# Attention ahead of a routed two-layer network: products with v later in the step, their diagonal part a step later, three probability buffers

## The chip, the cores and the metric

One Trainium2 chip, one of its cores. The metric is device time in microseconds (us) of one execution. TensorE (PE, with its weight loads as PEld), VectorE (DVE), ScalarE (ACT) and GpSimd (POOL) each run their instructions in the order in which they were issued; SyncE (SP) and the queues of ACT and POOL issue transfers (DMA). The order on each engine is written out by hand; waits between engines are semaphores.

## The reference

```python
def _attn_ref(q, k, v):                    # q, k, v: 8 batches, 8 heads, 576 rows, 64 wide
    scores = 1.0 / np.sqrt(D) * np.matmul(q, k.transpose(0, 1, 3, 2))
    mask = block_i >= block_j              # blocks of 64 rows
    scores = np.where(mask, scores, -1000000000.0)
    attn = np.exp(scores - np.max(scores, axis=-1, keepdims=True))
    attn = attn / (np.sum(attn, axis=-1, keepdims=True) + 1e-09)
    return np.matmul(attn, v)

def _moe_ref(x, domain_id, w1, w2):        # x: 4608 x 512, 8 experts, 512 -> 1024 -> 512
    for e in range(E):
        mask = domain_id == e
        out[mask] = np.maximum(x[mask] @ w1[e], 0.0) @ w2[e]
    return out
```

The attention's output, laid out as 4608 rows of 512, is x of the second part.

## The kernel before

**Pairs.** The 64 heads are worked in 32 pairs (two heads, t = 0 and 1, side by side on 64 partitions each); four pairs are a batch. Of a pair, the scores are made transposed (keys on partitions) in three groups of one PSUM tile `ps` each (two buffers, two banks each): G0, G1 and G2 (`emit_G0`, `emit_G1`, `emit_G2`), each followed by one exp on ACT (`emit_exp`, L375) that writes 1024 columns of f16 probabilities into the buffer `A` of the pair (two buffers, `As`). G0 holds the keys of block column 0, G1 those of 1, G2 those of 2 and 3; the tail (rows 512 to 575 against keys 512 to 575, a 64 x 64 product for each head, L386) is written into G0's tile.

**Products with v.** `emit_P` (L412) makes 20 products of 128 x 128 probabilities with 65 columns of v (the first column is ones, so the sums come out as well) into the PSUM tile `po`; `emit_D` (L424) makes the 10 products of the diagonal blocks: 8 of 64 x 64 and, last, two of the tail (64 x 128). `emit_N` (L433, L434) divides on DVE out of `po` into `x`; `store_x` (L443, L444) sends x to `xd` in DRAM, once a batch, and for the last batch in two pieces.

**Turning q and k.** q and k are loaded as they lie (`load_qk`, four buffers, POOL's queue) and turned on PE by 18 transposes for two pairs of one of them (`emit_T`, L359) into the PSUM tile `PT` (one buffer), which DVE copies (L362) into `QK` (two buffers).

**Order.** In the loop `for p in range(npair + 1)` PE gets, in step p: G1(p), P(p - 1), D(p - 1), G2(p), G0(p + 1), and then one T; DVE gets the division of pair p - 1, the copy of T and one piece of `routing()`, the work that sorts the rows by expert. In step 23 the sorting's last products (`inv_mm`, 36 of them, L220) and `inv_close` stand after G0. The v and q, k of later batches are asked for in the first step of a batch.

**Into the second part.** Weights are loaded from step 22 on by the same POOL queue. `early_gather` (steps 24 to 26 and 28 to 30) fetches rows of x that lie in the first five batches for the first two experts; `early_block` (steps 30, 31 and 32, L476, into `PT`) turns the three blocks of the first expert. After the loop `mm1` (L601) and `mm2` (L618) work the experts one by one; the rest of the rows (`gather`, L462) is fetched when all of x has been stored. `transpose_block` turns these blocks, and everything after them follows on PE.

Of the kernel before, what the change touches and what calls it, by code (L numbers as in the profile page):

```python
# [17 lines left out]
def kernel(  # L18
# [10 lines left out]
    nc = tc.nc  # L29
# [34 lines left out]
    kh = [asb.tile([128, HP, S], F16, name=f"kh{i}") for i in range(RV)]  # L64
    As = [asb.tile([128, 2, 64 + 3 * 512], F16, name=f"A{i}") for i in range(2)]
    vS = [asb.tile([128, 5, H, 80], F16, name=f"vS{i}") for i in range(RV)]
# [93 lines left out]
    for i in range(RV):  # L160
        nc.vector.memset(vS[i][:, :, :, 15:16], 1.0)
    for i in range(2):
        nc.vector.memset(As[i][:, :, 0:64], 0.0)

# [167 lines left out]
    def new_QK(G):  # L332
        QKs[G] = asb.tile([128, 2, 2, S], F16, name="QK", tag="QK", bufs=2)

# [44 lines left out]

    def emit_G0(st):  # L380
        ps, QK, i = new_ps(), st["QK"], st["i"]
        st["A"] = As[st["p"] % 2]
# [8 lines left out]
    def emit_G1(st):  # L391
        ps = new_ps()
        mm_qk(ps[:, :, 0:64], st, 0, 512, 576)
        mm_qk(ps[:, :, 64:512], st, 1, 128, 576)
        emit_exp(st["A"][:, :, 576:1088], ps[:])
# [10 lines left out]
    def emit_P(st):  # L406
        b = st["p"] // HP
        for w in range(4):
            for t in range(2):
                for c in range(w + 1):  # L410
                    n0 = (128, 576, 896, 1088)[c] + 128 * w
                    nc.tensor.matmul(  # L412
                        out=po[:, t, 65 * w : 65 * w + 65],
                        lhsT=st["A"][:, t, n0 : n0 + 128],
                        rhs=vS[b % RV][:, c, head(st, t), 15:80],
                        start=(w == 0), stop=False)

    def emit_D(st):
        b = st["p"] // HP
        for w, c, n0, k in ((0, 1, 640, 0), (1, 2, 1088, 0), (2, 3, 1408, 0),  # L420
                            (4, 0, 64, 0), (3, 4, 0, 64)):
            r0 = 0 if k else 64
            for t in range(2):
                nc.tensor.matmul(  # L424
                    out=po[r0:128, t, 65 * w : 65 * w + 65],
                    lhsT=st["A"][k : k + 64, t, n0 : n0 + 128 - r0],
                    rhs=vS[b % RV][k : k + 64, c, head(st, t), 15:80],
                    start=False, stop=(w == 3))

    def emit_N(st):  # L430
        c0 = 256 * (st["p"] % HP // 2)
        rc = asb.tile([128, 2, 5], F32, name="rc", tag="rc", bufs=2)
# [22 lines left out]
    def new_pair(p):  # L455
        st = {"p": p, "i": p % 2, "QK": QKs[p // 2]}
        emit_G0(st)
        return st
# [43 lines left out]
    new_QK(1)  # L502
    T_ahead = {0: (1, 0)}
    T_mid = {1: (1, 1)}
    T_end = {}
    for p in range(1, npair):
        G = (p + 3) // 2
        if G < npair // 2:
            T_end[p] = (G, 1 - p % 2)
    prev = None  # L510

    def tok_of(e):
        return tok0[:, :, NB * e : NB * e + NB]

    for p in range(npair + 1):
        b, hp = divmod(p, HP)
        st, nxt = nxt, None
        if st is not None:
            if hp == 0:
                x_t = asb.tile([128, 5, DM], F16, name="x", tag="x", bufs=2)  # L520
            st["x"] = x_t
            emit_G1(st)
        if prev is not None:
            emit_P(prev)
        if p in T_mid:
            emit_T(*T_mid[p])
        if prev is not None:
            emit_D(prev)
        if st is not None:
            emit_G2(st)  # L530
            if p in T_ahead:
                emit_T(*T_ahead[p])
            if p + 1 < npair:
                nxt = new_pair(p + 1)
        if prev is not None:
            emit_N(prev)
            if prev["p"] == npair - 2:
                store_x(prev, 0, DM - 192, nc.sync)
            elif prev["p"] == npair - 1:
                store_x(prev, DM - 192, DM, nc.scalar)  # L540
            elif prev["p"] % HP == HP - 1:
                store_x(prev, 0, DM, nc.sync)
        if p == 1:
            next(rout)
        if p == 23:
            pv = po[:, 0, 325 : 325 + 2 * E * NB].rearrange("p (a c) -> p a c", a=2)
            inv_mm(inv, pv)
            inv_close(asb, pv, E * NB, tok0[:])
        if p in T_end:
            G, s = T_end[p]  # L550
            if s == 0 and G > 1:
                new_QK(G)
            emit_T(G, s)
        if hp == 0 and 1 <= b < B - 3:
            load_v_chunks(b + 3, 0, H, range(5))
        if p >= 1 and hp == (b == 0) and b + 4 < B:
            load_qk(b + 4, 0, HP)
        if p > 1:
# [179 lines left out]
```

## Time and profile before

| | |
|---|---|
| median of 3 runs | 279.83 us (279.24 to 280.53) |
| the profiled execution | 280.8 us, its span 278.7 us |
| busy in the span | PE 255.0 (91%), PEld 167.1, DVE 136.6, ACT 140.2, POOL 157.4 us |
| mean granted TensorE clock | 0.97 of full speed |
| POOL's DMA queue | 59936 packets, 45.63 MB, 96.3% of 16 engines' span |

A span is the time from the first to the last instruction. The attention fills the first 117 us, with ACT, DVE and PE all busy nine tenths of the time; from 130 us on PE alone is busy, without a gap until the last expert. Idle time of an engine counts where the next work waits for it; the view of an engine in order of time gives, in brackets, how long it stood before an instruction and what ended that.

### The profile page before, as it was taken

To read this page: it belongs to the slowest core of one execution; us is meant where nothing else is said; L and a number is where in the kernel's file an instruction comes from. 1 tells how busy PE (TensorE), PEld (TensorE's weight loads), DVE (VectorE), ACT (ScalarE), POOL (GpSimd) and SP (SyncE) were. 2 spreads that over 40 slices of the span, in tenths; PEclk is the share of its full clock that TensorE was granted. 3 is DMA by queue.
4 is the path that set the end of the run, shared out by engine and by line. 5 is a ranking of instruction groups with operands and counts; after the bars stand their busy time and mean duration, and the time that the engine had idled before them with its cause. 6 is when DMAs were issued, how large, how long until landed. Compare 5 with 4: busy or idle time off the path is not lost. (4 is left out here: it accounts for less than half of the span.)

```text
span 278.7 us, 7091 instructions
## 1 busy us (share of the span) xinstructions
PE 255.0 (91%) x3010; PEld 167.1 (60%) x3010; DVE 136.6 (49%) x257; ACT 140.2 (50%) x170; POOL 157.4 (56%) x184
## 2 busy tenths in 40 slices
PE   7599999999999998797999999999999999999940
PEld 5367766777776776554675575665755656657410
DVE  4657999999997976404133404214033042250220
ACT  1747989999997899450352160340521604406200
POOL 8696474553635463108748767687776877051240
PEclk9858999999999999999999999999999999999995
DMA  6999999999999999954997999999999996021030
GB/s 85 153 151 170 193 220 194 216 204 194 225 181 229 186 236 248 238 151 83 201 263 155 211 252 217 278 161 243 223 223 281 189 228 250 25 110 59 38 136 2
DMA packets 65585, 50.86 MB, mean 183 GB/s; under 512 B 40973, under 2 KB 53773, under 8 KB 65552
## 3 DMA queue, kind: packets, MB, share of 16 engines
q0 software_dynamic: 59936, 45.63, 96.3%
q1 hardware_dynamic: 5088, 4.56, 6.0%
q8 instruction: 25, 0.41, 0.5%
q10 hardware_dynamic: 528, 0.20, 0.3%
q14 instruction: 8, 0.07, 0.1%
HBM read 67.15 MB, written 15.20 MB: 296 GB/s over the span
## 5 line engine op out<-in xcount | busy, mean ns | idle before, releaser
L375 ACT ACTIVATE A<-ps 128x1024 f16<-128x1024 f32 x96 | 91.9, 1024 | 15.2 <-PE ps L370 13.4
L605 ACT ACTIVATE hT<-ph 128x640 f16<-128x640 f32 (+2 forms) x72 | 46.4, 644 | 98.6 <-PE ph L601 94.9
L618 PE MATMUL po<-w2h,hT 128*128 128x512 f16 x320 | 74.9, 379 | 0.0
L601 PE MATMUL ph<-xT,w1h 128*128 128x320 f16 (+2 forms) x512 | 71.8, 299 | 1.3 <-DVE xT L479 1.2
L601 PEld LDWEIGHTS <-w1h 128*128 128x128 f16 x512 | 50.0, 98 | 22.8 <-issue 2.4
L628 POOL DMA_INDIRECT out_dram<-osb,tok x40 | 40.4, 1010 | 35.1 <-DVE osb L627 22.5
L479 DVE COPY xT<-pt 128x512 f16<-128x512 f16 x37 | 15.5, 424 | 89.2 <-PE pt L476 89.2
L462 POOL DMA_INDIRECT xg<-x_rows,tok x34 | 34.3, 1010 | 25.3 <-DMA x_rows<-x 12.1
L618 PEld LDWEIGHTS <-hT 128*128 128x128 f16 x320 | 29.9, 98 | 29.5
L94 POOL DMA_DIRECT2D vS<-in_v_dram x40 | 33.2, 839 | 20.1 <-DMA kh<-in_k_dram 8.5
L362 DVE COPY QK<-PT 128x1152 f16<-128x1152 f16 x30 | 40.7, 1356 | 6.8 <-PE PT L359 5.4
L370 PE MATMUL ps<-QK 64*128 64x512 f16 (+4 forms) x320 | 38.6, 300 | 4.0 <-ACT A L375 1.8
L627 DVE COPY osb<-po 128x512 f32<-128x512 f32 x40 | 27.4, 684 | 19.4 <-PE po L618 19.4
L412 PE MATMUL po<-vS,A 128*128 128x65 f16 x640 | 26.4, 198 | 1.4 <-DVE x L434 0.8
L412 PEld LDWEIGHTS <-A 128*128 128x128 f16 x640 | 22.5, 100 | 8.6 <-issue 6.8
L434 DVE TENSOR_TENSOR x<-po,rc 128x640 f16<-128x640 f32 x32 | 26.4, 824 | 1.1
L370 PEld LDWEIGHTS <-QK 64*128 64x128 f16 x320 | 16.8, 95 | 11.5 <-issue 6.0
L424 PE MATMUL po<-vS,A 64*64 64x65 f16 (+1 forms) x320 | 20.0, 199 | 0.0
L476 PEld LDWEIGHTS <-xg 128*128 128x128 f16 x160 | 11.7, 98 | 9.5 <-DMA xg<-x_rows,tok 2.4
L424 PEld LDWEIGHTS <-A 64*64 64x64 f16 (+1 forms) x320 | 14.5, 108 | 3.3 <-issue 0.2
L476 PE MATMUL pt<-identh,xg 128*128 128x128 f16 x148 | 14.0, 219 | 2.0 <-DMA xg<-x_rows,tok 2.0
L123 POOL DMA_DIRECT2D w1h<-in_moe_w_dram x16 | 12.2, 766 | 5.8 <-PE ph L601 2.6
(98 smaller groups left out, 140.4 us busy)
## 6 DMA issues: line engine op xcount, KB each, us to landing
w1h<-in_moe_w_dram POOLq DMA_DIRECT2D x16, 512.0 KB, 7.9
w2h<-in_moe_w_dram POOLq DMA_DIRECT2D x16, 512.0 KB, 10.2
vS<-in_v_dram POOLq DMA_DIRECT2D x28, 128.0 KB, 11.8
x_rows<-x SPq DMA_DIRECT2D x7, 512.0 KB, 10.9
qh<-in_q_dram POOLq DMA_DIRECT2D x6, 576.0 KB, 13.8
kh<-in_k_dram POOLq DMA_DIRECT2D x6, 576.0 KB, 13.8
vS<-in_v_dram POOLq DMA_DIRECT2D x16, 64.0 KB, 7.4
qh<-in_q_dram POOLq DMA_DIRECT2D x3, 288.0 KB, 6.9
```

Of the source, the lines that this page charges most:

```text
L94: nc.gpsimd.dma_start(out=vS[b % RV][r0:128, c, h0:h1, 16:80], in_=v[b, h0:h1, 128 * c : 128 * c + n, :].rearrange("h p d -> p h d"))
L362: nc.vector.tensor_copy(out=QKs[G][:, s].rearrange("p i (n j) -> p i n j", j=R), in_=P16.rearrange("p (j i n) -> p i n j", j=R, i=2))
L370: nc.tensor.matmul(out=o[:, t], lhsT=QK[h, 1, i, 128 * c : 128 * c + 128], rhs=QK[h, 0, i, q0:q1], start=True, stop=True)
L375: nc.scalar.activation(out=o, in_=i, func=AF.Exp, scale=0.125)
L412: nc.tensor.matmul(out=po[:, t, 65 * w : 65 * w + 65], lhsT=st["A"][:, t, n0 : n0 + 128], rhs=vS[b % RV][:, c, head(st, t), 15:80], start= ...
L424: nc.tensor.matmul(out=po[r0:128, t, 65 * w : 65 * w + 65], lhsT=st["A"][k : k + 64, t, n0 : n0 + 128 - r0], rhs=vS[b % RV][k : k + 64, c, ...
L462: nc.gpsimd.indirect_dma_start(out=g[:, blk, :], out_offset=None, in_=xd, in_offset=bass.IndirectOffsetOnAxis(ap=tok[:, 1, blk : blk + 1], ...
L601: nc.tensor.matmul(out=ph[:, i, 0:w], lhsT=w1_cols(w1h, dc, fc), rhs=xT[:, dc, c0 : c0 + w], start=(dc == 0), stop=(dc == 3))
L605: nc.scalar.activation(out=hT[:, fc, n0 : n0 + k * w].rearrange("p (i n) -> p i n", i=k), in_=ph[:, 0:k, 0:w], func=AF.Relu)
L618: nc.tensor.matmul(out=po[:], lhsT=hT[:, fc, 128 * blk : 128 * blk + 128], rhs=w2h[:, fc, :], start=(fc == 0), stop=(fc == 7))
L627: nc.vector.tensor_copy(out=osb[:], in_=po[:])
L628: nc.gpsimd.indirect_dma_start(out=dst[blk], out_offset=bass.IndirectOffsetOnAxis(ap=tok[:, 0, blk : blk + 1], axis=0), in_=osb[:], in_off ...
```

## The change

The products with v of pair p - 1 (P) move from between G1(p) and G2(p) to behind G0(p + 1); their diagonal part (D) and the division move into the step after: the two tail products open the step, ahead of G1, and the eight diagonal ones follow G1. The tail scores move from G0's tile into G1's, right ahead of the diagonal products; G0 takes columns 64 to 575 and G1 the first 64. T moves from the end of the step to between the diagonal products and G2. `As` and `QK` get a third buffer. The loop has one step more, the division and each `store_x` come a step later, the loads of v, q and k are asked for in the second step of a batch, `early_block` stands in steps 29 to 31, behind P. The last pair's output lies in `PT` rather than `po`, with a memset of its unused corner.

PE, in a step of the steady loop, before, from the transposes T on (kh, qh: loaded k and q; QK: turned; A: probabilities; equal rows between are left out):

```order
L359 MATMUL PT<-identh,kh_78 64x128
L370 MATMUL ps<-QK 128x64
...
L370 MATMUL ps<-QK 128x448
L412 MATMUL po<-vS_84,A_80 128x65
...
L424 MATMUL po<-vS_84,A_80 64x65
...
L424 MATMUL po<-vS_84,A_80 128x65
L370 MATMUL ps<-QK 128x320
...
L370 MATMUL ps<-QK 128x512
L386 MATMUL ps<-QK 64x64
```

and with the change:

```order
L412 MATMUL po<-vS_84,A_82 128x65
...
L423 MATMUL po<-vS_84,A_82 128x65
L370 MATMUL ps<-QK 128x64
...
L370 MATMUL ps<-QK 128x448
L392 MATMUL ps<-QK 64x64
L423 MATMUL po<-vS_84,A_82 64x65
...
L359 MATMUL PT<-identh,qh_74 64x128
...
L370 MATMUL ps<-QK 128x320
...
L370 MATMUL ps<-QK 128x512
L412 MATMUL po<-vS_84,A_80 128x65
```

P has left the place between G1 (128x448) and G2 (128x320); there now stand the tail scores, the diagonal products and T.

PE, at the end of the attention, before, from G2 of the last pair on (xg: fetched rows that `early_block` turns; w1h: weights of the first expert):

```order
L370 MATMUL ps<-QK 128x192
L476 MATMUL PT<-identh,xg 128x128
L412 MATMUL po<-vS_85,A_81 128x65
...
L424 MATMUL po<-vS_85,A_81 64x65
L424 MATMUL po<-vS_85,A_81 128x65
...
L476 MATMUL PT<-identh,xg 128x128
L601 MATMUL ph<-xT,w1h 128x384
```

and with the change:

```order
L370 MATMUL ps<-QK 128x192
L412 MATMUL po<-vS_86,A_80 128x65
...
L479 MATMUL PT<-identh,xg 128x128
L423 MATMUL po<-vS_86,A_80 128x65
L423 MATMUL po<-vS_86,A_80 64x65
L412 MATMUL PT<-vS_86,A_81 128x65
L423 MATMUL PT<-vS_86,A_81 128x65
L423 MATMUL PT<-vS_86,A_81 64x65
L612 MATMUL ph<-xT,w1h 128x384
```

Two pairs' products with v now stand behind the last G2, and the last block to be turned stands between them.

The core of the diff:

```diff
@@ buffers
-    As = [... for i in range(2)]          QK bufs=2
+    As = [... for i in range(3)]          QK bufs=3
@@ emit_G0, emit_G1
     def emit_G0(st):
-        mm_qk(ps[:], st, 0, 0, 512)
-        (two tail products into ps[64:128, t, 0:64])
-        emit_exp(st["A"][:, :, 64:576], ps[:])
+        mm_qk(ps[:], st, 0, 64, 576)
+        emit_exp(st["A"][:, :, 0:512], ps[:])
     def emit_G1(st):
-        mm_qk(ps[:, :, 0:64], st, 0, 512, 576)
+        mm_qk(ps[:, :, 0:64], st, 0, 0, 64)
         mm_qk(ps[:, :, 64:512], st, 1, 128, 576)
+        (two tail products into ps[64:128, t, 0:64])
         emit_exp(st["A"][:, :, 576:1088], ps[:])
@@ emit_D(st, parts)
+    D_last = ((3, 4, 512, 64),)
+    D_diag = ((0, 1, 640, 0), (1, 2, 1088, 0), (2, 3, 1408, 0), (4, 0, 576, 0))
@@ the loop
-    for p in range(npair + 1):
+    for p in range(npair + 2):
+        if pp is not None:
+            emit_D(pp, D_last)
         if st is not None:
             emit_G1(st)
-        if prev is not None:
-            emit_P(prev)
-        if prev is not None:
-            emit_D(prev)
+        if pp is not None:
+            emit_D(pp, D_diag)
+            emit_N(pp)
+            (store_x of pp as before of prev)
+        turn_qk(p, 0)
         if st is not None:
             emit_G2(st)
             if p + 1 < npair:
                 nxt = new_pair(p + 1)
-        if prev is not None:
-            emit_N(prev)
         (p == 23: inv_mm, inv_close)
-        if p in T_end:
-            emit_T(G, s)
-        if hp == 0 and 1 <= b < B - 3:
-            load_v_chunks(b + 3, 0, H, range(5))
+        if prev is not None and p > 1:
+            if p == npair:
+                prev["po"] = new_PT()[0].rearrange("p (t c) -> p t c", t=2)
+                nc.vector.memset(prev["po"][0:64, :, 260:325], 1.0)
+            emit_P(prev)
+        if hp == 1:
+            if 1 <= b < B - 3:
+                load_v_chunks(b + 3, 0, H, range(5))
+            if b + 4 < B:
+                load_qk(b + 4, 0, HP)
-        if 30 <= p < 30 + NE:
-            early_block(p - 30, new_PT()[0][:, 0:256])
-        prev = st
+        if 29 <= p < 29 + NE:
+            early_block(p - 29, new_PT()[0][:, 0:256])
+        prev, pp = st, prev
```

## Rows read from the trace of the kernel before

**Rows 1.** ACT in order of time: start, length, instruction, [idle before, releaser].

```profile
34.98 2.85 ACT L375 ACTIVATE A<-ps 128x1024 f16<-128x1024 f32 x3 [0.19 <-PE ps L370]
...
62.91 2.86 ACT L375 ACTIVATE A<-ps 128x1024 f16<-128x1024 f32 x3 [0.19 <-PE ps L370]
...
81.19 2.86 ACT L375 ACTIVATE A<-ps 128x1024 f16<-128x1024 f32 x3 [0.19 <-PE ps L370]
...
107.53 2.85 ACT L375 ACTIVATE A<-ps 128x1024 f16<-128x1024 f32 x3 [0.19 <-PE ps L370]
```

**Rows 2.** PE in order of time, one step; columns as in rows 1.

```profile
63.09 0.22 PE L386 MATMUL ps<-QK 64*64 64x64 f16 x2
63.24 0.69 PE L359 MATMUL PT<-identh,qh 128*64 128x128 f16 x18
63.98 0.40 PE L370 MATMUL ps<-QK 64*128 64x64 f16 x4
64.31 0.79 PE L412 MATMUL po<-vS,A 128*128 128x65 f16 x20
65.03 0.58 PE L424 MATMUL po<-vS,A 64*64 64x65 f16 x9
65.42 0.31 PE L370 MATMUL ps<-QK 64*128 64x320 f16 x1
```

**Rows 3.** Busy time by stretch: stretch, length, engines, granted clock, DMA share, GB/s.

```profile
13.00:22.00 9.00, 8.05 (x109) 5.98 (x109) 4.76 (x10) 4.44 (x5) 8.72 (x12) 0.50 1.41 155
24.00:60.00 36.00, 34.82 (x700) 25.42 (x696) 33.89 (x55) 33.20 (x36) 19.27 (x24) 1.00 1.67 199
```

**Rows 4.** Issues on POOL, SP and ACT in order of time; columns as in rows 1.

```profile
23.23 0.74 POOL L75 DMA_DIRECT2D kh<-in_k_dram  x1 [0.66 <-DMA qh<-in_q_dram]
...
63.91 0.76 POOL L75 DMA_DIRECT2D qh<-in_q_dram  x1
...
79.59 0.59 SPq L444 DMA_DIRECT2D x_rows<-x  x1
...
95.31 1.09 POOL L488 DMA_INDIRECT xg<-x_rows,row  x1 [0.66 <-DVE rc L433]
...
116.94 0.41 ACTq L444 DMA_DIRECT2D x_rows<-x  x1
```

**Rows 5.** Transfers of single stretches: what, queue, count, KB each, us to landing.

```profile
kh<-in_k_dram POOLq DMA_DIRECT2D x1, 576.0 KB, 11.5
...
qh<-in_q_dram POOLq DMA_DIRECT2D x1, 576.0 KB, 15.1
...
x_rows<-x SPq DMA_DIRECT2D x7, 512.0 KB, 10.9
...
xg<-x_rows,row POOLq DMA_INDIRECT x1, 13.5
...
x_rows<-x ACTq DMA_DIRECT2D x1, 192.0 KB, 7.3
...
xg<-x_rows,tok POOLq DMA_INDIRECT x4, 2.8
```

**Rows 6.** PE in order of time, from the attention's end into the experts.

```profile
110.91 0.40 PE L476 MATMUL PT<-identh,xg 128*128 128x128 f16 x4
...
114.47 0.78 PE L412 MATMUL po<-vS,A 128*128 128x65 f16 x20 [0.62 <-DVE x L434]
...
117.29 5.63 PE L601 MATMUL ph<-xT,w1h 128*128 128x384 f16 x32 [1.17 <-DVE xT L479]
...
127.90 0.40 PE L476 MATMUL pt<-identh,xg 128*128 128x128 f16 x4 [0.86 <-DMA xg<-x_rows,tok]
129.45 0.40 PE L476 MATMUL pt<-identh,xg 128*128 128x128 f16 x4 [1.15 <-DMA xg<-x_rows,tok]
```

**Rows 7.** PE early in the attention, in order of time.

```profile
11.19 0.69 PE L359 MATMUL PT<-identh,qh 128*64 128x128 f16 x18 [1.58 <-DMA qh<-in_q_dram]
...
20.33 1.28 PE L412 MATMUL po<-vS,A 128*128 128x65 f16 x20
```

More of the change, by code (lines that the diff above doesn't have):

```diff
@@ L64 @@
     kh = [asb.tile([128, HP, S], F16, name=f"kh{i}") for i in range(RV)]
-    As = [asb.tile([128, 2, 64 + 3 * 512], F16, name=f"A{i}") for i in range(2)]
+    As = [asb.tile([128, 2, 64 + 3 * 512], F16, name=f"A{i}") for i in range(3)]
     vS = [asb.tile([128, 5, H, 80], F16, name=f"vS{i}") for i in range(RV)]
@@ L161 @@
         nc.vector.memset(vS[i][:, :, :, 15:16], 1.0)
-    for i in range(2):
-        nc.vector.memset(As[i][:, :, 0:64], 0.0)
+    for i in range(3):
+        nc.vector.memset(As[i][:, :, 512:576], 0.0)
     def slot_col(sb, r_f, d_f, w, u, nm):
@@ L332, in new_QK @@
     def new_QK(G):
[L333 removed]
+        QKs[G] = asb.tile([128, 2, 2, S], F16, name="QK", tag="QK", bufs=3)
     def emit_T_first(i):
@@ L416, in emit_P, with emit_D @@
                         start=(w == 0), stop=False)
-    def emit_D(st):
+    def emit_D(st, parts):
         b = st["p"] // HP
-        for w, c, n0, k in ((0, 1, 640, 0), (1, 2, 1088, 0), (2, 3, 1408, 0),
-                            (4, 0, 64, 0), (3, 4, 0, 64)):
+        for w, c, n0, k in parts:
             r0 = 0 if k else 64
@@ L502, with turn_qk @@
     new_QK(1)
[L503 to L506, printed above, removed]
+    Ts = {(0, 1): (1, 0), (1, 0): (1, 1), (1, 2): (2, 0)}
+    for p in range(2, npair):
         G = (p + 3) // 2
         if G < npair // 2:
-            T_end[p] = (G, 1 - p % 2)
-    prev = None
+            Ts[p, 0] = (G, 1 - p % 2)
+    def turn_qk(*at):
+        if at in Ts:
+            G, s = Ts[at]
+            if s == 0 and G > 1:
+                new_QK(G)
+            emit_T(G, s)
+    prev = pp = None
     def tok_of(e):
         return tok0[:, :, NB * e : NB * e + NB]
-    for p in range(npair + 1):
+    for p in range(npair + 2):
         b, hp = divmod(p, HP)
@@ L521 @@
             st["x"] = x_t
+        if pp is not None:
+            emit_D(pp, D_last)
+        if st is not None:
             emit_G1(st)
-        if prev is not None:
-            emit_P(prev)
-        if p in T_mid:
-            emit_T(*T_mid[p])
-        if prev is not None:
-            emit_D(prev)
+        if pp is not None:
+            emit_D(pp, D_diag)
+            emit_N(pp)
+            if pp["p"] == npair - 2:
+                store_x(pp, 0, DM - 192, nc.sync)
+            elif pp["p"] == npair - 1:
+                store_x(pp, DM - 192, DM, nc.scalar)
+            elif pp["p"] % HP == HP - 1:
+                store_x(pp, 0, DM, nc.sync)
+        if p == 1:
+            next(rout)
+        turn_qk(p, 0)
         if st is not None:
             emit_G2(st)
-            if p in T_ahead:
-                emit_T(*T_ahead[p])
+            turn_qk(p, 1)
+            if p == 1:
+                emit_P(prev)
+                turn_qk(1, 2)
             if p + 1 < npair:
                 nxt = new_pair(p + 1)
-        if prev is not None:
-            emit_N(prev)
[L537 to L544, printed above, removed]
         if p == 23:
```

27 lines of the change are left out of this document (12 added, 15 removed).

## The prediction

> **What bounds the kernel now.** I read ACT in order of time first, because the attention is 117 us of 280.8 and ends it. From 62.91 to 81.19 the last exp of a step starts every 3.05 us (18.28 over 6 steps), three exps take 2.85 and ACT stands 0.19, each time for TensorE (PE), which is late with the scores G2 [rows 1]. So PE sets the pace by a loop, read off PE in order of time: exp of G2 at 62.91, G1 at 63.98, P 64.31, D 65.03, G2 65.42, next exp 65.96 [rows 1, 2]. From 81.19 to 107.53 there are 8 steps and 1.95 more, the sorting's products in step 23 [rows 1]. ACT's three exps without the wait are a floor of about 2.85 a step, and DVE, busy 33.89 us of 36.00 from 24 to 60 [rows 3], needs some 2.87: 0.94 of 3.05. At most 0.2 a step is to be had.
>
> The second view is the loads. POOL's transfers are a stream of their own: DMA works all the time, the turned q and k wait for nothing in the steady steps only because they have lead. The third is PE behind the attention: mm1 at 117.29, then waits for fetched rows of 0.86 and 1.15 [rows 6], from there no gap; what is late at 127.9 and 129.5 is therefore late at the end, one for one.
>
> **The steady step.** Between G1 and G2, 1.44 us now (63.98 to 65.42), stand P and D [rows 2]. With the change there stand the tail scores, eight diagonal products and T. Priced from the same step: G1 0.33 (its start to that of P). A change of tile shape 0.12: from 63.09 to 63.24 PE makes two small tail products and turns to T, and 0.15 is far more than the products. Ten small products, two of the tail scores and eight of D, 0.28: D has 0.39 from start to start, less a change 0.27, over 9. T 0.47: its 0.69 less the overlap of a row with the next, 0.2 as D's 0.58 has over its 0.39. Two changes, D to T and T to G2, 0.27. That is 1.35 instead of 1.44, and the last two products no longer stand between D and G2 (0 to 0.05). The tails share the tile shape of the diagonal products, so a step has five changes of shape for six. I take **0.13 a step**, the middle of 0.09 and 0.18 (the latter is the ACT and DVE floors, 3.05 less 2.87). P lies behind G0 while ACT has two exps to do; its cover is the exp of G2 and G0, and it costs only if its division is late. The third A and QK cost nothing in the loop: what fills them are the same exps and copies. The memset of a third A, at the start, stands beside the loads that PE waits for (1.58 at 11.19, [rows 7]); without that cover it is a fraction of a us.
>
> **What T's new place costs.** T was behind G2 by 0.33 after its exp's start (62.91 to 63.24); now G2 stands behind T, so T starts about 1.15 before the exp. A load that came at T's time with 1.5 of room less is now on the path. k of batch 2 was asked for at 23.23, took 11.5 and had landed at 34.7; exp G2 of step 6 was at 34.98 and can now not be before 34.7 + 1.15 = 35.9: **+0.9** [rows 1, 4, 5]. q of batch 6: asked at 63.91, 15.1 us, landed 79.0, so step 21's exp is not before 80.2, against 81.19: **-1.0** there [rows 1, 4, 5]. The pace alone would have brought it to 81.19 + 0.9 - 15 x 0.13 = 80.1, so this load hardly adds. POOL asks a step later in the text for v, q and k, but it stands for room in its queue and not for the kernel (0.66 for a transfer before 23.23), so I put that at nothing; if the cover is missing, at one step, 3 us, of a load's lead. `store_x` a step later: batch 4's was issued at 79.59 and takes 10.9; at 82.6 it would land at 93.5, still ahead of the gather at 95.31 [rows 4, 5]. Step 23: P(22) now stands behind the sorting's products and waits for their readers, about 0.5, in place of a wait of like length; nothing either way. At step 29 I have 81.19 - 80.2 = 1.0 and 8 x 0.13 more, **2.1 gained**: exp G2 at 105.4 instead of 107.53.
>
> **The gathered rows.** Here the gain goes. `early_block` now comes in step 29, behind P. Its first rows are asked for at 95.31 and take 13.5 us: they land at 108.8 [rows 4, 5]. Before, PE turned them at 110.91, 2.1 later, with no wait [rows 6]. Now PE would be ready about 1.0 after exp G2, at 106.4, and stands there **2.4 us** for them. This transfer is behind the weights in its queue, and the queue's place does not move with the kernel (no row shows one that does). So at 108.8 PE is where it was before, or later:
>
> - first block 0.40 [rows 6], G1(30) at 109.25, exp G2(30) 1.9 later (1.98 in rows 1 and 2, less 0.1) at 111.1, exp G2(31) at 114.0; before 107.53 + 2 x 3.05 = 113.62.
> - behind G2(31) there now stand P(30), a block, D(30), its division, P(31), D(31), its division. Before, P(31) stood 0.62 for a division and the last store left 2.47 after it (114.47 to 116.94) [rows 4, 6]. Now P(30) waits for one division (0.6 to 0.9), P(31) for the next and for the memset of its PSUM tile that DVE has behind it: I take twice 0.62, 1.3. P, a block and D are 0.72 + 0.40 + 0.58. G2(31) at 113.5, P(30) 113.8 + 0.7, D(30) ends 115.8 to 116.0, P(31) about 117.0, last store **119.5** against 116.94: +2.6.
>
> **From the last store to the end.** It took 7.3 us to land beside the weights (116.94 to 124.24), and a gather with nothing beside it takes 2.8 [rows 4, 5]. Issued later, when more of the weights are through, it lands after 2.8 to 7.3; I take the middle, 5.05, at 124.55, 0.3 later than before. The fetched blocks follow it by the same 3.7 and 5.2 us, and the end follows them: **+0.3**; at the upper end +2.6, of which I count +1.5, since the weights that slowed it come to their end in those 2.6 us. At the lower end PE itself is late: mm1 needs the PSUM tile that the last pair now uses, 1.6 later, against 0.86 + 1.15 of waits that shrink first [rows 6], so no more than **-0.5** can come.
>
> What the Trainium skill says of this, "DMA: Bandwidth & Descriptors", section "Queues, rings and completion order", is that an engine takes turns between queues. By it a store of 192 KB would get its share of each engine at once, and land near the lower end, which would make the sum -0.5. The 7.3 row speaks against a fast landing beside the weights; no row shows the store alone.
>
> Profiled, 280.8 + 0.3 = 281.1; the profiled run lies 0.97 above the median of 279.83, so **280.1**. By the bounds -0.5 to +1.5 and a little for the steps, 279.3 to 281.6 is its own range.
>
> **Rivals.**
>
> *A, slower: PE's clock falls at the gather.* From 13 to 22 the granted clock is 0.50 of 2.4 GHz, the lower level, after PE had stood 1.58 for q [rows 3, 7], and 20 products of P took 1.28 there and 0.79 at full clock [rows 2, 7]. In the forecast PE stands 2.4 at 106.4, longer than that, then again about 0.8 and 1.3. If the clock falls there, steps 30 and 31 with their tails run their PE parts at 1.6 times: some 4 us of PE work until the last store become 6.4, of which waits hide a part; the store goes 2 later, and mm1's first share (5.63) is stretched too. Range +0.5 to +3.7, I take +2.8: **282.6**. It decides once PE stands at the first block about as long as at 11.19. Against it: up to 22 the lower clock followed a start with other waits for loads, and here PE comes out of a stretch at 1.00 (24 to 60) [rows 3].
>
> "TensorE: Matmul & The Clock Gate", Part 1, in the Trainium skill has the lower level as what the engine falls back to without sustained activity. [...]
>
> *B, faster: loads and gathers move with the kernel.* If the requests are early because POOL or the readers that free its buffers were early, the first block is ready when PE is, and the pace is kept: 27 steps of 0.13 are 3.5, the two waits for divisions and the memset take 2.2 and the last blocks' waits may take a little off, so -1.3 to -2.2: **278.2**. For it: the gather at 95.31 stood for DVE (0.66), which would be earlier [rows 4]. Against it: the transfer's 13.5, five times an unloaded one.
>
> *C, the change doesn't do what it says:* the turn of PE's shape costs as much elsewhere and the step stays 3.05. Then PE meets the gather at 108.5, stands 0.2 or so, and the last store is at 119.5 all the same: **280.1**.
>
> **Chances.** Forecast 0.38, A 0.32, B 0.20, C 0.10. 0.5% is 1.4 us, about what a measurement of this kernel can tell from none. Within it: 0.32 of the forecast, 0.04 of A, 0.03 of B, 0.08 of C: 0.47. Faster: 0.17 of B and 0.03 of the forecast's: 0.20. Slower: 0.28 of A, 0.03 of the forecast, 0.02 of C: 0.33. The range reaches from B (278.2 and 0.3 more) to A's 280.3 to 283.5, a little short of its end: 277.9 to 283.2, with perhaps 0.07 below and 0.06 above.
>
> **What would show it.** Pace: the last exp of a step every 2.9 in 62 to 80, idle before it 0.05 to 0.1 instead of 0.19; a pace of 3.05 is C. T's place: in steps 5 or 6 and 20 or 21 a wait of PE before the transposes, named after kh or qh. The gate: PE idle some 2.4 before the first block's transposes, xg named; none, or below 0.5, is B. The clock: a stretch 105 to 120 below 1.00 is A. The tail: last store at 119.5, landing 3 to 7 later, the wait before the fetched blocks near 0.86 again or gone. I would be wrong above all if a transfer that I hold fixed in time, of q, k or the gather, moves with the step.

## The result, and the profile with the change

The changed kernel takes 284.35 us (median of 4 runs, 283.64 to 284.53) where the kernel before, beside it, takes 280.18: a ratio of 1.0137, interval 1.0098 to 1.0175. It is slower by 4.2 us by these medians, by 3.8 by the ratio. The forecast was 280.1 with a range of 277.9 to 283.2; the time lies 1.15 above the range, and the sign is that of rival A. In the ratios here and below, runs over 1.5% above the fastest of the same kernel are left out.

The profiled execution has a span of 282.2, against 278.7. The mean granted clock of TensorE is 0.95 (0.97 before).

ACT in order of time, with the change, where rows 1 stand for before (start, length, instruction, idle before and releaser):

```profile
56.38 17.51 ACT L375 ACTIVATE A<-ps 128x1024 f16<-128x1024 f32 x18 [0.29 <-PE ps L370]
74.64 13.66 ACT L375 ACTIVATE A<-ps 128x1024 f16<-128x1024 f32 x14 [0.74 <-PE ps L370]
...
111.27 2.93 ACT L375 ACTIVATE A<-ps 128x1024 f16<-128x1024 f32 x3 [3.69 <-PE ps L392]
115.21 1.94 ACT L375 ACTIVATE A<-ps 128x1024 f16<-128x1024 f32 x2 [1.01 <-PE ps L392]
121.91 0.41 ACTq L447 DMA_DIRECT2D x_rows<-x  x1
```

The steady steps did what was hoped for. Eighteen exps, six steps, take 17.51 with no gap of a size that the view shows: the 0.19 that ACT stood in each step [rows 1] no longer appear, and a step is 2.93 instead of 3.05 (some 0.07 over the 2.86 of three exps [rows 1]). The waits of 0.29 and 0.74 come in steps 13 and 19; ahead of the second, PE stood 0.45 in the midst of T (at 73.88), and the view names no load for either. Then ACT stands 3.69, another 1.01, and the last store (the ACTq row) leaves at 121.91, not at 116.94 [rows 4].

PE from the end of the attention on, with the change, where rows 6 stand for before:

```profile
105.80 0.39 PE L370 MATMUL ps<-QK 64*128 64x512 f16 x2 [0.52 <-ACT A L375]
106.12 0.79 PE L412 MATMUL po<-vS,A 128*128 128x65 f16 x20
109.72 0.61 PE L479 MATMUL PT<-identh,xg 128*128 128x128 f16 x4 [2.81 <-DMA xg<-x_rows,row]
...
112.34 0.61 PE L370 MATMUL ps<-QK 64*128 64x512 f16 x2 [0.19 <-ACT A L375]
112.89 1.28 PE L412 MATMUL po<-vS,A 128*128 128x65 f16 x20
113.98 0.60 PE L479 MATMUL PT<-identh,xg 128*128 128x128 f16 x4
...
116.54 0.78 PE L412 MATMUL po<-vS,A 128*128 128x65 f16 x20 [0.85 <-DVE x L437]
...
119.43 0.79 PE L412 MATMUL PT<-vS,A 128*128 128x65 f16 x20 [1.36 <-DVE PT L562]
...
121.93 6.35 PE L612 MATMUL ph<-xT,w1h 128*128 128x384 f16 x28 [0.29 <-DVE x L437]
128.12 1.89 PE L629 MATMUL po<-w2h,hT 128*128 128x512 f16 x8
```

PE stands 2.81 for the gathered rows of the first block (L479), 0.85 ahead of P(30) and 1.36 ahead of P(31), which waits for the memset of PT. P takes 1.28 at 112.89 and 0.79 at 106.12: between them the clock has gone to its lower level. The stretches of the three stands, busy time by stretch (PE, PEld, DVE, ACT, POOL, then the granted clock, DMA share, GB/s):

```profile
104.00:112.00 8.00, 4.57 (x66) 2.94 (x67) 2.13 (x8) 4.31 (x5) 2.31 (x3) 0.73 1.11 246
112.00:120.00 8.00, 5.61 (x101) 4.12 (x98) 3.90 (x9) 4.14 (x5) 1.48 (x2) 0.85 1.04 231
120.00:130.00 10.00, 9.63 (x61) 4.85 (x58) 1.05 (x2) 3.92 (x8) 3.28 (x4) 0.83 0.36 102
```

In the kernel before each of these three stretches has 1.00; the first two:

```profile
104.00:112.00 8.00, 6.92 (x122) 4.68 (x122) 5.00 (x11) 7.43 (x9) 3.22 (x5) 1.00 1.11 247
112.00:120.00 8.00, 6.21 (x90) 4.36 (x89) 2.75 (x6) 3.91 (x6) 0.96 (x1) 1.00 1.11 249
```

With the change the record of the clock has it at 0.50 from 107.6 to 114.4 and again from 121.3 to 124.7, over the first products of the experts.

A mark that both kernels pass behind all this is the first product of 320 columns, the second expert's. Before, with two stands on the way to it that rows 6 leave out:

```profile
108.60 0.40 PE L370 MATMUL ps<-QK 64*128 64x64 f16 x4 [0.68 <-ACT A L375]
...
111.65 0.40 PE L370 MATMUL ps<-QK 64*128 64x64 f16 x4 [0.35 <-ACT A L375]
...
139.39 6.82 PE L601 MATMUL ph<-xT,w1h 128*128 128x320 f16 x49
```

and with the change, with one stand ahead of the fetched blocks:

```profile
132.70 0.71 PE L479 MATMUL pt<-identh,xg 128*128 128x128 f16 x8 [0.29 <-DVE xT L482]
...
142.96 7.23 PE L612 MATMUL ph<-xT,w1h 128*128 128x320 f16 x52
```

It is 3.57 later, which is the difference of the spans (3.5). So all of the loss lies ahead of it, and the rest of the experts plays no part.

**Where it went.** The last exp of step 29 starts at 105.62 (107.53 before [rows 1]): 1.91 ahead. From there to the mark it is 37.34 against 31.86, 5.48 more. The stands with the change: 0.52 (of which 0.18 lies behind 105.62), 2.81, 0.19, 0.85, 1.36, 0.29 and, ahead of the blocks, 0.29 for DVE: 5.97. Before, over the same stretch: 0.68 and 0.35 for ACT, 0.62, 1.17, 0.86 and 1.15 [rows 6]: 4.83. That is 1.14 more. Lower clock: the experts' first group took 7.43 from 120.69 to 128.12, less its 0.29 of waiting, against 5.46 before, 1.68 more; the step from block to block (109.72 to 113.98) 4.26, of which 0.19 is a stand, against 3.05 in a run at full clock (busy_gate, below), of which 0.59 is one: 1.61 more. One P and its diagonal part, which the change puts off by half a step and more, so that they are not yet done at 105.62: 0.72 and 0.39, 1.11. Together 5.54, against 5.48. (Waits and lengths are known to about 0.1 each, so that the two meet this closely is luck.) Of the 1.91 that the steps seem to have won by then, 1.11 is therefore work that still has to come.

### The profile page after: what moved, and what is told of

It reads as the page before. It is cut to its first block, busy times and chain, and to the rows that moved or that the text cites. A ratio compares the mean times of both kernels' runs of the same rounds, so it can differ in the third digit from the quotient of the medians.

```text
span 282.2 us, 7084 instructions
## 1 busy us (share of the span) xinstructions
PE 255.4 (91%) x3010; PEld 164.1 (58%) x3010; DVE 136.1 (48%) x259; ACT 140.3 (50%) x170; POOL 157.5 (56%) x184
## 5 line engine op out<-in xcount | busy, mean ns | idle before, releaser
L612 PE MATMUL ph<-xT,w1h 128*128 128x320 f16 (+2 forms) x512 | 73.4, 302 | 0.5 <-DVE x L437 0.3
L370 PE MATMUL ps<-QK 64*128 64x64 f16 (+4 forms) x320 | 39.4, 308 | 3.4 <-ACT QK L349 0.8
L412 PEld LDWEIGHTS <-A 128*128 128x128 f16 x640 | 22.4, 100 | 10.2 <-issue 7.5
L412 PE MATMUL po<-vS,A 128*128 128x65 f16 x620 | 25.3, 197 | 1.2 <-DVE x L437 0.8
L437 DVE TENSOR_TENSOR x<-po,rc 128x640 f16<-128x640 f32 x31 | 25.6, 825 | 1.1
L370 PEld LDWEIGHTS <-QK 64*128 64x128 f16 x320 | 14.9, 96 | 12.9 <-issue 7.2
L423 PE MATMUL po<-vS,A 64*128 64x65 f16 (+1 forms) x310 | 20.8, 197 | 0.0
L479 PEld LDWEIGHTS <-xg 128*128 128x128 f16 x160 | 12.1, 100 | 10.2 <-DMA xg<-x_rows,row 2.9
L128 POOL DMA_DIRECT2D w2h<-in_moe_w_dram x16 | 12.0, 759 | 8.1 <-DMA w2h<-in_moe_w_dram 3.8
```

The costliest lines, as they stand in the source:

```text
L370: nc.tensor.matmul(out=o[:, t], lhsT=QK[h, 1, i, 128 * c : 128 * c + 128], rhs=QK[h, 0, i, q0:q1], start=True, stop=True)
L412: nc.tensor.matmul(out=st["po"][:, t, 65 * w : 65 * w + 65], lhsT=st["A"][:, t, n0 : n0 + 128], rhs=vS[b % RV][:, c, head(st, t), 15:80], ...
L423: nc.tensor.matmul(out=st["po"][r0:128, t, 65 * w : 65 * w + 65], lhsT=st["A"][k : k + 64, t, n0 : n0 + 128 - r0], rhs=vS[b % RV][k : k + ...
L612: nc.tensor.matmul(out=ph[:, i, 0:w], lhsT=w1_cols(w1h, dc, fc), rhs=xT[:, dc, c0 : c0 + w], start=(dc == 0), stop=(dc == 3))
```

## The experiments

The runs came in groups, each on one chip with the kernel before beside it. In two groups, that of busy_gate, busy_all, lastps and lastps_eb30 and that of best_w3late and before_w3late, all kernels, the one before too, took some 5 us more and scattered by 6 to 7; of these the traces say more than the times.

### Work of no use where PE stands: is it the clock?

The edit for busy_gate (the helper `keep_busy` is given the tile to write, which is left out here); busy_all has 7 and 12 more such products, into a free score tile, ahead of P(30) and P(31).

```diff
-            early_block(p - 29, new_PT()[0][:, 0:256])
+            bank = new_PT()[0][:, 0:256]
+            if p == 29:
+                keep_busy(24, bank)     # 24 products 128 x 256 of ones
+            early_block(p - 29, bank)
```

> The changed kernel, with 24 products of no use (128 x 256, about 2.6 us at full clock) into PT ahead of the first block's transposes in step 29, so that PE works while it waits for the gathered rows. Clock theory (PE's stand of 2.81 lets the clock fall from 107.6 to 114.4, and this costs time): clock 1.00 there, last exp of step 31 at 114.6 instead of 116.13, last store at 120.4 instead of 121.91, the second fall (121.3 to 124.7) stays; 282.9 us against 284.35. Rival (the clock falls but waits hide it, only the gate and the two waits for divisions cost): the store moves by under 0.5 and the time stays at 284 to 284.4.

Measured: 1.0136 over the kernel before (1.005 to 1.0223). The clock stayed at 1.00 at the gate, and from the last exp of step 29 to that of step 31 it took 8.85 (107.32 to 116.17) against 10.51 with the change (105.62 to 116.13): 1.66, where 1.5 was forecast. The time did not follow: 1.0136 is the changed kernel's own ratio, where 1.4 us less was expected. A fall came at 118.2, at the stand ahead of P(31), lasted to 125.1, longer than the changed kernel's second (121.3 to 124.7), and took the experts' first products with it.

> As busy_gate, and also 7 such products ahead of P(30) and 12 ahead of P(31), into a free score tile, where PE stood 0.85 and 1.36. Clock theory: neither fall is there, the first 28 products of the experts with the changed kernel's 6.35 take 4.8, and the time is 1.5 + 1.6 less than 284.35: 281.2. Rival (the second fall hides behind the fetched rows): as busy_gate, 282.9, with a new wait before the fetched blocks.

Measured: 1.0061 (1.0019 to 1.0104), no lower clock between 14.5 and 277. A quieter group has it again beside the changed kernel, in 12 runs each.

> The changed kernel with products of no use at the three stands (24, 7 and 12), once more beside the changed kernel on one chip. Clock theory: clock 1.00 from 30 on, 1.5 to 3 us under the changed kernel. Rival (the clock's fall is hidden): within 0.7 of it.

> The changed kernel unaltered, in as many rounds as busy_all2: 1.009 to 1.015 over the kernel before.

busy_all2 took 281.66 (280.25 to 282.75), after_5, the changed kernel, 283.94 (279.82 to 286.05). The medians are 2.3 apart, but the ratios to the kernel before are 1.0046 (1.0018 to 1.0074) and 1.0055 (1.001 to 1.010) and show no difference: that of after_5 rests on its six shorter runs, and its times go with the mean clock (279.82 came with 0.968, 284.17 and 285.82 with 0.939). So the times alone leave it open, and the traces must tell. That of after_5 is a run of 283.23; that of busy_all2 is its shortest, 280.25. PE of after_5, two rows:

```profile
107.77 0.61 PE L479 MATMUL PT<-identh,xg 128*128 128x128 f16 x4 [1.94 <-DMA xg<-x_rows,row]
...
142.00 8.86 PE L612 MATMUL ph<-xT,w1h 128*128 128x320 f16 x64
```

PE of busy_all2:

```profile
104.72 2.78 PE L156 MATMUL PT<-warm 128*128 128x256 f16 x24
107.47 0.40 PE L479 MATMUL PT<-identh,xg 128*128 128x128 f16 x4
...
139.23 8.86 PE L619 MATMUL ph<-xT,w1h 128*128 128x320 f16 x64
```

The first block is turned within 0.3 of the same time, yet the mark comes 2.77 earlier where PE was kept at work. Counted from the first block's start it is 31.76 against 34.23: **2.5 us is what two falls of the clock cost in after_5**, and 43 products of no use bring it back. The changed kernel unaltered was traced a third time (after_again, below), with nearly the same later stands (0.84 and 1.36) but with the first fall alone:

```profile
108.02 0.61 PE L479 MATMUL PT<-identh,xg 128*128 128x128 f16 x4 [3.30 <-DMA xg<-x_rows,row]
...
140.83 8.86 PE L612 MATMUL ph<-xT,w1h 128*128 128x320 f16 x64
```

So from the first block to the mark the changed kernel takes 32.81 with 6.8 us at the lower clock (after_again), 33.24 with 10.2 (the profile above) and 34.23 with 13.7 (after_5), and busy_all2 takes 31.76 with none: the distance grows with the time at the lower clock, in three traces of one kernel. In the profile above that makes the clock's share some 1.5 of the 3.5 (if anything more: the products of no use put P(30) 5.91 behind the first block, against 5.49 in busy_gate). It is less than the 1.61 and 1.68 counted above, since at full clock waits of 0.60, 0.42 and 0.71 come out from under the slower products.

### The gate alone, in the kernel before

```diff
-        if 30 <= p < 30 + NE:
-            early_block(p - 30, new_PT()[0][:, 0:256])
+        if 28 <= p < 28 + NE:
+            early_block(p - 28, new_PT()[0][:, 0:256])
```

> The kernel before with the first expert's blocks turned two steps earlier, in steps 28 to 30, and nothing else: the gate alone, without the change. PE reaches the first block at 105.5 and the rows land at 108.8, so it stands 3.3. Clock theory: the clock falls to 0.50 behind it, and the attention ends 4 to 5 us later; 0.9 + 1.15 of waits ahead of the fetched blocks take some of it back; the time is 2.5 to 4 us over the kernel before. Rival (a stand at that place is made up by waits behind it, or does not take the clock): under 1.5 us over it, clock 1.00.

Measured: 1.0136 over the kernel before (1.0049 to 1.0223). The trace is that of the longest of its four runs, 287.32, which the ratio leaves out; the three others took 282.62 to 286.58. PE, and a stretch behind it:

```profile
107.99 0.61 PE L476 MATMUL PT<-identh,xg 128*128 128x128 f16 x4 [2.71 <-DMA xg<-x_rows,row]
```

```profile
112.00:120.00 8.00, 7.97 (x91) 5.35 (x91) 2.59 (x9) 5.40 (x6) 2.04 (x2) 0.50 1.01 221
```

A stand of 2.71 at that place, in a kernel that has nothing else of the change, goes with the lower clock, here from 107.1 to 127.5. The three shorter runs, with mean clocks of 0.951 to 0.961, have no trace, so how long theirs lasted is not shown; but their ratio is that of the change. The blocks' place alone, ahead of the rows, is enough for a loss of that size.

### The end mended, with and without the gate

Three edits: the last pair's output into a free score tile, with the memset ahead of the division of pair 30; the last block turned ahead of P(30); the last store issued by SP. `best` has in addition `early_block` a step later.

```diff
+        if p == npair:
+            prev["po"] = new_ps()
+            nc.vector.memset(prev["po"][0:64, :, 260:325], 1.0)
...
-                store_x(pp, DM - 192, DM, nc.scalar)
+                store_x(pp, DM - 192, DM, nc.sync)
...
-        if 29 <= p < 29 + NE:
-            early_block(p - 29, new_PT()[0][:, 0:256])
+        if 30 <= p < 30 + NE:        # best_eb29: 29, as with the change
+            early_block(p - 30, new_PT()[0][:, 0:256])   # p == 31: ahead of P(30)
```

The first of the three alone, and that with the later blocks, ran first:

> The changed kernel with the last pair's output in a free score tile rather than in PT, and the memset of its corner ahead of the division of pair 30. The gate at step 29 stays. Expected where the wait for the memset counts: P(31) right behind D(30) at about 118.0 instead of 119.43, last store 0.9 earlier (DVE has two divisions in a row), experts from 119.3 instead of 120.69: 283.0; if with the wait gone the second clock fall goes too, 281.4. Rival (the end hangs on the last store alone): 0.9 or less, and a new wait before the fetched blocks.

> As lastps, with the first expert's blocks turned a step later, in steps 30 to 32, as in the kernel before. Gate theory: PE reaches the first block at about 108.6 and stands 1 us or less instead of 2.81, the clock stays at 1.00, last exp of step 31 at 111.6 to 112.6, last store at 116 to 117, time 277.5 to 279.5, faster than the kernel before by what is left of 1.9. Rival (the last stores and fetched rows land no earlier, whatever PE does): 279.5 to 280.5 with a wait of 2 or more before the fetched blocks.

Measured: 1.0009 (0.9956 to 1.0063) and 1.0011 (0.9958 to 1.0064), in the scattered group, where the gate of lastps was only 0.39. Neither kernel is shown to be faster than the one before, as the gate theory had wanted of the second, nor does the second have the wait ahead of the fetched blocks that its rival had. In neither trace did the clock fall between 27.5 and 276, although PE of lastps_eb30 stood for 2.05:

```profile
114.70 0.78 PE L412 MATMUL po<-vS,A 128*128 128x65 f16 x20 [2.05 <-DVE x L437]
```

In lastps P(31) no longer waits (0.16 for 1.36), but a new stand comes up. ACT in lastps, then PE:

```profile
119.23 0.41 ACTq L447 DMA_DIRECT2D x_rows<-x  x1
120.25 0.87 ACT L616 ACTIVATE hT<-ph 128x384 f16<-128x384 f32 x2 [4.56 <-DMA xg<-x_rows,row]
```

```profile
120.80 4.24 PE L612 MATMUL ph<-xT,w1h 128*128 128x384 f16 x24 [1.30 <-ACT hT L616]
```

ACT's first eviction of the experts stands behind the issue of the last store on the same engine and starts 1.02 after it; PE, which has two tiles only, waits 1.30 for it. Hence the move of that store to SP in the next pair.

> The changed kernel unaltered, so that the other runs of this group have it on their own chip: ratio to the kernel before 1.010 to 1.018 as in its first timing, PE standing 2 to 3 us for the gathered rows in step 29, clock 0.50 after it.

> The changed kernel with a mended end: the last pair's output in a free score tile with its memset ahead of the division of pair 30, the last block turned ahead of P(30), and the last store issued by SP instead of ACT (where the experts' evictions stand behind it). The gate in step 29 stays. Gate theory: PE still stands 2 to 3 us there and the clock falls; the last store comes at 118 to 119.5 and the time is 1 to 3 us under the changed kernel's, about that of the kernel before. Rival (the end alone made the loss, the gate costs nothing): already as fast as best, 276.5 to 278 if before is at 280.

> As best_eb29, with the first expert's blocks turned one step later, in steps 30 to 32. Gate theory: PE stands under 1 us at the first block, clock 1.00 throughout, last exp of step 31 at 111.5, last store at 115 to 116, time 2 to 4 us under the kernel before and 1.5 to 3 us under best_eb29. Rival (the fetched rows set the end): no more than 1 us under the kernel before, with 2 us or more of waits ahead of the fetched blocks.

Measured, on one chip: after_again 1.010 (1.0037 to 1.0164), with a stand of 3.30 and the clock at 0.50 from 106.3 to 113.2; best_eb29 1.0017 (0.9982 to 1.0053), 281.49, with a stand of 1.79 and the clock at 0.50 from 109.2 to 122.9; best 1.0037 (1.0006 to 1.0068), 281.91. Mending the end gives back most of the loss by these ratios, whose intervals just overlap. PE of best_eb29:

```profile
108.54 0.40 PE L479 MATMUL PT<-identh,xg 128*128 128x128 f16 x4 [1.79 <-DMA xg<-x_rows,row]
...
141.34 8.86 PE L614 MATMUL ph<-xT,w1h 128*128 128x320 f16 x64
```

From the first block to the mark it takes 32.80 with 13.7 us at the lower clock, where after_5 takes 34.23 with as much: some 1.4 us lie in the end, beside what lies in the clock. Taking the gate away as well gives nothing more, against what was expected, though in best everything ahead of the stores is as hoped: clock 1.00, last exp of step 31 at 110.29, last store out at 115.13, 1.8 earlier than in the kernel before. SP and POOL in best:

```profile
115.13 0.59 SPq L447 DMA_DIRECT2D x_rows<-x  x1
```

```profile
124.10 0.99 POOL L465 DMA_INDIRECT xg<-x_rows,tok  x1 [12.31 <-issue]
```

and PE:

```profile
126.89 0.55 PE L479 MATMUL pt<-identh,xg 128*128 128x128 f16 x4 [3.03 <-DMA xg<-x_rows,tok]
128.33 0.61 PE L479 MATMUL pt<-identh,xg 128*128 128x128 f16 x4 [0.89 <-DMA xg<-x_rows,tok]
```

The gather of the late rows is issued at 124.10. In the kernel before it was 125.11:

```profile
125.11 1.00 POOL L462 DMA_INDIRECT xg<-x_rows,tok  x1 [12.14 <-DMA x_rows<-x]
```

It was 125.81 with the change, where the store left at 121.91. Whether the last store leaves at 115 or at 122, the gather starts at 124 to 126: the store takes 8.1 in best and 3.1 with the change. What PE wins in the attention it stands out ahead of the fetched blocks (3.03 and 0.89), and behind that stand the clock falls again, from 127.0 to 133.8. The rival won.

### What the late rows wait for

Ahead of the last stores, POOL has asked for 2 MB of the second expert's weights. In the next runs these stand behind the gathers.

```diff
-        if p == 27:
-            for f in weights(1):
-                f()
...
     for e in range(2):
         gather(xgs[e], tok_of(e), range(NE, NB))
+    for f in weights(1):
+        f()
     for f in weights(2):
         f()
```

> As best, with the second expert's weights (2 MB, four loads) asked for behind the gathers of the late rows instead of in step 27. Backlog theory (in best the last stores, issued by 115.1, landed at 123.2, because the transfers asked for before them kept DMA busy until then): the stores land at 117.5 to 119, the gather is issued at 118 to 120 instead of 124.1, the waits of 3.03 and 0.89 ahead of the fetched blocks are gone, and the time is 4 to 5.5 us under the kernel before, 275 to 276.5 where before is at 280.4. Rival (a store takes 8 us there for another reason): gather still at 123 or later and about the time of best, 281 to 282.

Measured: 1.0164 (1.0129 to 1.02). The last store's transfer in best, then in best_w1late (what, queue, count, KB, us to landing):

```profile
x_rows<-x SPq DMA_DIRECT2D x1, 192.0 KB, 8.1
```

```profile
x_rows<-x SPq DMA_DIRECT2D x1, 192.0 KB, 2.5
```

POOL and PE of best_w1late:

```profile
118.15 0.99 POOL L465 DMA_INDIRECT xg<-x_rows,tok  x1 [9.77 <-DMA x_rows<-x]
```

```profile
133.45 8.86 PE L611 MATMUL ph<-xT,w1h 128*128 128x320 f16 x64
150.21 0.61 PE L479 MATMUL pt<-identh,xg 128*128 128x128 f16 x4 [7.91 <-DMA xg<-x_rows,tok]
```

The backlog theory holds: the store lands in 2.5, the gather is issued six us earlier, and the mark comes at 133.45, 5.9 ahead of the kernel before. But now two sets of weights stand ahead of the third expert's rows, and PE waits 7.91 for those. The same edit to the two kernels:

> The kernel before with only that: the second expert's weights behind the gathers. Backlog theory: the last store, at 116.9, lands at 119 to 120.5 instead of 124.2, the waits of 0.86 and 1.15 go and no more, since PE is then the last: 1.5 to 2.2 us under the kernel before. Rival: no difference (within 0.7).

> The changed kernel with only that. Here PE has no wait for fetched blocks, it is late itself, so an earlier gather gives nothing: within 1 us of the changed kernel's first ratio, 1.010 to 1.014 over the kernel before. The gate stays, since its rows are asked for before those weights. Rival (the changed kernel too is held by the fetched rows): 3 us or more under it.

Measured: 1.0253 (1.0217 to 1.029) and 1.0425 (1.037 to 1.048), both far slower than any theory had it, with 5.03 and 5.68 of waiting at that same place and the lower clock behind it. What was expected of the first expert came true (no wait ahead of its fetched blocks); the third expert's rows had not been thought of. (A short fall, 118.9 to 122.3, came in before_w1late even with the stands of 0.62 and 1.17 that left the clock alone in the kernel before.)

So in best_w2late and before_w2late the third expert's weights go behind its gathers as well, and in best_w3late and before_w3late every later set too.

> As best_w1late, but the third expert's weights stand behind the third expert's gathers too, so that those are not held up (there PE waited 7.91 for them at 150). Backlog theory: the experts' first product of 320 columns starts at 133 to 134 as in best_w1late (139.4 in the kernel before), no wait over 1 us behind it, and the time is 4 to 6 us under the kernel before. Rival (the transfers are a fixed sum and a later expert waits instead): within 1 us of it or over.

> The kernel before with the same order of weights and gathers and nothing else. Backlog theory: the waits of 0.86 and 1.15 go, 1.5 to 2.2 us under the kernel before; best_w2late stays 2.5 to 4 us under this one, which is the pace gain. Rival: the weights alone make the gain, and this one comes within 1 us of best_w2late.

Measured: 1.0031 (0.999 to 1.0073) and 1.0087 (1.0049 to 1.0126); before_w2late has no wait for the late rows either, but one of 2.42 at 167.7, behind which the clock stays at 1.00. PE of best_w2late:

```profile
134.29 8.86 PE L611 MATMUL ph<-xT,w1h 128*128 128x320 f16 x64
...
165.11 0.61 PE L479 MATMUL pt<-identh,xg 128*128 128x128 f16 x4 [3.52 <-DMA xg<-x_rows,tok]
```

The mark is 5.1 ahead of the kernel before, and the fourth expert's rows take it back: 3.52 and the lower clock from 164.0 to 170.9. The rival (a later expert waits instead) came true.

> As best_w2late, but from the second expert on every set of weights is asked for right behind the gathers of the expert it belongs to, so that no gather stands behind two sets of weights (in best_w2late PE waited 3.52 at 165 for the fourth expert's rows, and the clock fell). Theory (the step gain is real and reaches the end once no transfer is in the way): the first product of 320 columns at 134 to 135, no wait for rows over 0.5 behind it, clock 1.00 from 30 to 270, and 4 to 6 us under the kernel before: 274.5 to 276. Rival (transfers as a sum bind the experts too): another wait turns up and the time is within 1.4 us of the kernel before.

> The kernel before with that order of gathers and weights and nothing else: the waits of 0.86 and 1.15 go, the first product of 320 columns at 137.5 to 138 (139.4 before), 1.4 to 2.2 us under the kernel before, and 3 to 4 us over best_w3late, which would be the share of the changed steps with a mended end. Rival (the order of the weights makes the whole gain): within 1 us of best_w3late.

Measured, in a scattered group again (before: 283.07 to 288.79): 0.9981 (0.9938 to 1.0024) and 0.9882 (0.9791 to 0.9974). The second is below 1 by its interval, but that rests on two of its six runs, and the median of the six is that of the kernel before (285.65 and 285.63). In best_w3late no wait for rows is left and the clock stays at 1.00 from 22.5 to 275.1; its mark is at 136.8, and the time behind it is lost in stands of 0.9 to 1.9 us, three of the four for ACT, that are not in the quieter groups' traces. This pair settles nothing. No version was shown to be faster than the kernel before.

### The tail scores put back

The edit in short (the columns of A that P and D read move with it):

```diff
 emit_G0:   mm_qk(ps[:], st, 0, 0, 512), then the two tail products; exp into A[:, :, 64:576]
 emit_G1:   mm_qk(ps[:, :, 0:64], st, 0, 512, 576), without tails
```

> The changed kernel with the tail scores back in G0's tile, behind G0's products; all else as changed. Theory (a change of tile shape costs about 0.12 of PE, and the step has one more): last exp of a step every 2.98 to 3.05 us where the changed kernel has 2.93. Rival (the gain comes from P's and T's places alone): 2.93 or less, since two products less stand between G1 and G2.

Measured: 1.0105 over the kernel before (1.0051 to 1.0159), two runs. ACT in tails_G0:

```profile
49.81 5.75 ACT L375 ACTIVATE A<-ps 128x1024 f16<-128x1024 f32 x6 [0.23 <-PE ps L370]
55.78 5.75 ACT L375 ACTIVATE A<-ps 128x1024 f16<-128x1024 f32 x6 [0.22 <-PE ps L370]
61.76 5.75 ACT L375 ACTIVATE A<-ps 128x1024 f16<-128x1024 f32 x6 [0.23 <-PE ps L370]
```

Two steps take 5.98 (49.81 to 55.78 to 61.76), so 2.99 a step, with 0.23 of standing in every second one. Before it was 3.05, with the change 2.93: half of the 0.12 comes from the tails' place; the rest must lie in those of P and T, which no run moves alone. "TensorEngine Tiling (Array Packing)" in the Trainium skill says under "Key Properties" that a change of the tiling mode drains TensorE; 0.06 a step for one change less agrees with that, and it is half of the 0.12 that I had taken for one; the run moves the two tail products too, so that 0.06 is the price of the place as a whole.

## Why the prediction was wrong, by its own steps

- **The step's pace: right.** 0.13 a step was forecast, 0.12 measured. G1, the tail scores, D and T were priced at 1.35 together, and in the changed kernel G2 follows G1 by 1.36 (63.32 to 64.68). In tails_G0 one change of shape more made 0.06 a step, half of what I took for one.
- **The loads: right in kind.** Exp of step 6 at 35.39 (35.9 forecast), of step 21 at 80.50 (80.2), of step 29 at 105.62 (105.4). There were small waits at steps 5, 13 and 19 that the two rows did not show; the first is for a load of q (0.51 at 31.35), what the other two were for is not shown.
- **The gate: right.** 2.4 forecast, 2.81 measured. The rows were asked for at 95.03 and took 14.6 (95.31 and 13.5 before [rows 4, 5]): they did not move with the kernel, and came 0.8 later though the last exp of step 29 was 1.9 earlier. The waits for the division (0.6 to 0.9) and the memset (1.3) were 0.85 and 1.36.
- **The clock: the step that failed.** The forecast let PE stand 2.4, 0.8 and 1.3 and kept the clock up. I had the row against it, a fall behind a stand of 1.58 [rows 3, 7], gave rival A 0.32, and spoke against it with the long stretch at 1.00 that came before. That stretch did not protect it: the clock fell with the stand of 2.81 here, with 2.71 in before_gate and with 3.03 in best, each time after 80 us or more at full clock. With the clock kept up (busy_all2) the kernel is 1.3 us over the kernel before by its ratio, 1.6 by the medians, which is about the upper end of the forecast's own -0.5 to +1.5; with it down the time left the range. "TensorE: Matmul & The Clock Gate", Part 1, in the Trainium skill, calls the lower level the default that only activity lifts. The falls above agree with that; but a stand of 1.79 went with a fall in best_eb29, and 2.05 in lastps_eb30 and 2.42 in before_w2late with none, so the length of a stand alone did not decide it here.
- **Rival A's size.** +2.8 was taken, up to +3.7; on the profiles it is +3.5, on the medians +4.2. It had the store 2 later (121.5; it was 121.91), but one fall only. The second, from 121.3, behind 0.85 and 1.36, made the experts' first products 1.7 longer; in after_again the same stands brought none. The range was cut below A's own upper end, and the time lies past both.
- **From the store to the end.** I took a middle of 5.05 for the landing; it was 3.1, so the gather left only 0.7 later than before, and there is no wait ahead of the fetched blocks. It was PE that was late: the forecast had the experts start 1.6 later, under the 2.0 of those waits; they started 3.4 later (120.69) and, with the second fall, ended their first group 5.4 later (128.12 against 122.75). On the profiles the miss is 3.2 (+3.5 against +0.3); by my estimate 1.5 of it is the clock, 0.8 the later rows at the gate, and the rest this lateness of PE, which I had hidden under the waits. Where 7.3 had been read as the store's own, the runs show what it is: the end of a backlog at 123 to 124, whether the store left at 115.13 (best) or 116.94 (before). With the weights in that order, a last store 1.8 earlier brought the gather forward by 1.0 (124.10 in best, 125.11 before); so rival B's 278.2 seems out of reach unless the backlog ended earlier too, which no run with this order of the weights shows. The sentence from "DMA: Bandwidth & Descriptors", by which engines take turns between queues, had put the store near the lower end; with 2 MB of weights in the other queue the 192 KB took 8.1, without them 2.5, so turns alone did not make this small transfer quick.

What stays open: whether the steps' gain can be carried to the end by another order of gathers and weights. best_w1late and best_w2late had 5 to 6 us at the mark and lost them to the next transfer; best_w3late, which should have kept them, ran where differences under 1% can't be told.

## What to carry to other kernels

A stand of PE of two or three us can cost its own length and as much again, since the clock can go down with it (in after_5 a stand of 1.94 at the gate, and 2.5 by two falls); price both, with a chance for the fall, since stands of 2.05 and 2.42 went without. Ask of each planned wait what PE can do meanwhile (43 products of no use brought the 2.5 back). When a stretch is made faster, look first for the transfers that do not move with it: here the gathered rows at the gate and the backlog ahead of the last gather fixed both ends, and 0.12 in each of 27 steps passed neither. Work that is put off by half a step makes a step look faster than the stretch is, so count what is still to come at the mark where you compare.

## What the runs showed of the hardware that was not expected

- The lower clock came twice within 14 us with the change (107.6 to 114.4, 121.3 to 124.7), the second time behind stands of 0.85 and 1.36. The same kernel with stands of 0.84 and 1.36 kept 1.00 there in after_again, and fell from 116.8 to 123.6 in after_5: equal stands had unequal ends. In the kernel before, 0.86 and 1.15 left the clock alone [rows 6].
- The first evictions of the experts were held by the issue of a store ahead of them on ACT: 1.02 from the store's row to the next ACTIVATE, though the row itself is 0.41 long.
- 192 KB from SBUF to DRAM took 8.1, 7.3, 3.1 and 2.5 us in four kernels, by what POOL's queue still had to move; with the weights ahead of it, its end moved by 1.0 (123.2 and 124.2) when it was asked for 1.8 earlier (best and before).
